# Chunked attention feeding a token and channel mixer: the loads of later q, k and v, the pairs' weight ring and the weights' sums move from SyncE's queue to ScalarE's

## The chip, the cores and the metric

The kernel runs on one core of a Trainium2 chip. The metric is the device time of one execution in microseconds (us), as the median of several runs. Below, PE is TensorE (PEld its weight loads), DVE is VectorE, ACT is ScalarE, POOL is GpSimd and SP is SyncE, which in this kernel issues DMAs and computes nothing.

## The reference

The batch is 8, with 8 heads, 576 positions and a head dimension of 64. Attention is taken within chunks of 64 positions, and its result is the input x (8 x 576 x 512) of a mixer without normalisation:

```python
scores = scale * np.matmul(q_c, k_c.transpose(0, 1, 2, 4, 3))   # chunks of 64
scores = scores - np.max(scores, axis=-1, keepdims=True)
attn = np.exp(scores)
attn = attn / (np.sum(attn, axis=-1, keepdims=True) + 1e-09)
out = np.matmul(attn, v_c)
...
xt = x.transpose(0, 2, 1)
h = np.maximum(xt @ w_tok1, 0.0) @ w_tok2        # 576 -> 256 -> 576
u = x + h.transpose(0, 2, 1)
h2 = np.maximum(u @ w_ch1, 0.0) @ w_ch2          # 512 -> 1536 -> 512
return (u + h2).astype(np.float32)
```

## The kernel before

**Precision.** Every operand of the mixer is held as a high part (a cast to the fast 32-bit matmul type) and a low part (what the cast left out), and each product is three matmuls: high x high, low x high, high x low. So a cast on ACT (`xh`, `rh`, `gh`, `bh`) is always followed by a subtraction on DVE or POOL (`xl`, `rl`, `gl`, `bl`).

**Stages.** The 4608 columns (batch x position) go through the channel MLP in blocks: first two halves of batch 0, then two single blocks of 512 columns, then three pairs of blocks. A pair uses a scheme with 7 products instead of 8, which needs sums and differences of the first channel weights. These sums are made on POOL (`add_sums`, L1017, into the one buffer `sparts`), split into high and low (`split_sums`: ACT L1023, POOL L1024), written to HBM as `w<-sparts` (`dump`, L881) and read back in the pairs through a ring of eight buffers (`load_product`, `ring<-w`, L1041), one load for each product on PE (L1051).

**Attention beside it.** The attention of later tiles (128 positions, 8 heads each) is cut into bursts that are put between the matmuls of the single blocks and of the first pairs. For one tile: `qk` and `v` are loaded (L304, L315) two bursts ahead; PE makes the scores (L372, beside the output product L384 of the tile two bursts earlier); DVE subtracts the maximum (L345, L348), ACT takes the exponential (`pr`, L352), DVE transposes 32 x 32 blocks (`blocks`, L395), and SP writes them to HBM (`far<-blocks`, L400) and reads them back rearranged (`pf<-far`, four DMAs, L406). ACT copies them to `pt` (L423), the weights of the output product L384. The tile's output x goes the same way: it is cast to `xh` (L483) and `xl` (POOL L484) for the token MLP (L581, `ps_t`; ACT `rh` L599, DVE `rl` L600; L653), and as blocks through HBM to `xt` (L406), the residual that DVE adds into `u` (L660).

**What sets the order.** PE's order and SP's order are written out by hand (SP issues in the order of the code). ACT, DVE and POOL are ordered by a scheduler, and some instructions are pinned behind another with `tc.issue_after`. All DMAs of the program, whoever issues them, take eight completion semaphores in turn; the issue of a DMA waits until the DMA eight places earlier, which holds the same semaphore, has landed.

Of the kernel before, what the change touches and what calls it, by code (L numbers as in the profile page):

```python
# [8 lines left out]
F32 = mybir.dt.float32  # L9
# [51 lines left out]
DUMPS = 2  # L61
# [46 lines left out]
def attention_mixer_kernel(ctx, tc, qk_in, vo_in, v_in, w1_in, w2_in, wc1_in, wc2_in, out):  # L108
# [19 lines left out]
    nc = tc.nc  # L128
# [170 lines left out]
            xts[k] = pool.tile([P, N // BK, NDT, BK], F32, tag="xt", name="xt")  # L299
        return xts[k]  # L300

    def load_qk(i):
        qk = pool.tile([P, 2, NHP, P], F32, tag="qk" if i > 4 else "qk0", name="qk", bufs=3 if i > 4 else 5)
        nc.sync.dma_start(out=qk.rearrange("p a b c -> p (a b c)"), in_=qk_in[i])  # L304
        tiles[i] = {"qk": qk}

    def load_v(i):
        if i < NTILE:
            v = pool.tile([P, VPAD], F32, tag="v1" if i > 4 else "v0", name="v", bufs=2 if i > 4 else 5)
            v = v[:, :VW].rearrange("p (a b c) -> p a b c", a=2, c=DV)  # L310
            src = vo_in[i]
        else:
            v = pool.tile([P, 2, NHP, D], F32, tag="v", name="v", bufs=4)
            src = v_in[i - NTILE]
        nc.sync.dma_start(out=v.rearrange("p a b c -> p (a b c)"), in_=src)  # L315
        tiles[i]["v"] = v

    def attn_load(i):
        load_qk(i)
        load_v(i)  # L320

    def attn_s(i, src=None, tag="at"):
        t = tiles[i]
# [17 lines left out]
    def attn_p(i, fill=0):  # L341
        t = tiles[i]
        sv = t["s"]
        mx = per_row("mx")
        nc.vector.tensor_reduce(out=mx, in_=sv, axis=AX.X, op=ALU.max)  # L345
        convert(fill)
        pr = t["pr"] = pool.tile([P, DM], F32, tag="pr", name="pr")
        nc.vector.tensor_tensor(  # L348
            out=pr.rearrange("p (h a k) -> p a h k", a=2, k=CH), in0=sv,
            in1=mx.broadcast_to([P, 2, NHP, CH]), op=ALU.subtract,  # L350
        )
        nc.scalar.activation(out=pr, in_=pr, func=AF.Exp, scale=1.0 / float(D) ** 0.5)  # L352

    def attn_z(i):

        t = tiles[i]
        zi = t["zi"] = per_row("zs")
        nc.vector.tensor_reduce(
            out=zi, in_=t["pr"].rearrange("p (h a k) -> p a h k", a=2, k=CH), axis=AX.X, op=ALU.add
        )  # L360
        nc.scalar.activation(out=zi, in_=zi, func=AF.Copy, bias=1e-9)
        nc.vector.reciprocal(out=zi, in_=zi)

    def attn_both(i, j):

        ps = ps_at.tile([P, 2, 512], F32, tag="at", name="ps_sv")
        if i is not None:
            qk = tiles[i]["qk"]
            for hp in range(NHP):
                for a in range(2):  # L370
                    for c in range(2):
                        nc.tensor.matmul(  # L372
                            ps[c * CH:(c + 1) * CH, a, hp * CH:(hp + 1) * CH],
                            lhsT=qk[a * D:(a + 1) * D, 0, hp, c * CH:(c + 1) * CH],
                            rhs=qk[a * D:(a + 1) * D, 1, hp, c * CH:(c + 1) * CH],
                            start=True, stop=True,
                        )
            tiles[i]["s"] = ps[:, :, :NHP * CH].rearrange("p a (h k) -> p a h k", k=CH)
        if j is not None:
            t = tiles[j]  # L380
            for hp in range(NHP):
                for a in range(2):
                    for c in range(2):
                        nc.tensor.matmul(  # L384
                            ps[c * CH:(c + 1) * CH, a, (NHP + hp) * D:(NHP + hp + 1) * D],
                            lhsT=t["pt"][a * CH:(a + 1) * CH, hp, c * CH:(c + 1) * CH],
                            rhs=t["v"][a * CH:(a + 1) * CH, c, hp, :D],
                            start=True, stop=True,
                        )
            t["pv"] = ps[:, :, NHP * D:2 * NHP * D].rearrange("p a (h d) -> p a h d", d=D)  # L390

    def far_out(src, tag="far"):

        blocks = pool.tile([P, DM], F32, tag="blocks", name="blocks")
        nc.vector.transpose(  # L395
            out=blocks.rearrange("p (g n c) -> p n g c", g=4, c=BK),
            in_=src.rearrange("p (n g c) -> p n g c", g=4, c=BK),
        )
        far = dram.tile([P, DM], F32, tag=tag, name="far", bufs=4 if tag == "far" else 24)
        nc.sync.dma_start(out=far, in_=blocks)  # L400
        return far
# [66 lines left out]
    def attn_end(i):  # L468
        t = tiles[i]
        if i % NTILE == 4 and i > 4:  # L470
            attn_stack(i)
        t["own"] = t["x"]
        t["x"] = far_out(t["x"], "far_x")
        close_tile(i)
# [12 lines left out]
    def batch_split(b):  # L487

        for t, _, _ in mix_tiles(b):
            attn_split(t)  # L490
            stack_end(t)
# [54 lines left out]
    def load_waiting(n):  # L546

        while waiting and n > 0:
            n -= load_x(*waiting.pop(0))
# [8 lines left out]
    def batch_tiles(b):  # L558
        base = (b // 2) * NTILE
        return [base + j for j in (range(0, 5) if b % 2 == 0 else range(5, 9))]  # L560
# [251 lines left out]
    for engine in engines:  # L812
        ins = [i for i in nc.cur_bb.bb.instructions if i.engine == engine][-1]
# [4 lines left out]
    order = [t for b in range(2, B) for t in sorted(batch_tiles(b), key=lambda t: t % NTILE != 4)]  # L818
# [55 lines left out]
    wide = ctx.enter_context(tc.tile_pool(name="wide", bufs=1, space=bass.MemoryType.DRAM))  # L874
    stored, tokens, dumps = {}, {}, []

    def dump(n):

        for key, src in dumps[:n]:
            stored[key] = wide.tile([P, 2, KH], F32, tag="w{}_{}".format(*key), name="w")  # L880
            nc.sync.dma_start(out=stored[key], in_=src if src.dtype == F32 else src.bitcast(F32))  # L881
        del dumps[:n]

# [47 lines left out]
    def attention(k):  # L931

        i = order[k] if k < len(order) else None
        j = order[k - LAG] if k >= LAG else None
        attn_both(i, j)
        if k + 2 < len(order):
            attn_load(order[k + 2])
        load_waiting(1)
        if i is not None:
            attn_p(i)  # L940
            tiles[i]["far"] = far_out(tiles[i]["pr"])
            attn_z(i)
        ready = len(waiting)
        if j is not None:
            attn_o(j)
            attn_end(j)
        load_waiting(min(2, ready))
# [88 lines left out]
    products = [(p, n) for _ in range(PAIRS) for p in range(NFC // 2) for n in range(7)]  # L1036

    def load_product(upto):
        for i in range(len(ring), min(upto, len(products))):
            w = pool.tile([P, 2, KH], F32, tag="ring", name="ring", bufs=RING)  # L1040
            nc.sync.dma_start(out=w, in_=stored[products[i]])  # L1041
            ring.append(w)

    def product(i, u, width):
# [211 lines left out]
    for k in range(SINGLE):  # L1256
        at, width = BLOCKS[k]
        accs, pend = [], None
        for f in range(NFC):
            for half in range(2):  # L1260
                if half == 0:
                    g = ch1(u, f, width=width)
                elif pend is not None:
                    ch2(*pend)
                if half == 1:
                    pend = (S + at, width, u, f, g, accs)
                now = 2 * (NFC * k + f) + half
                if now in TOKENS_AT:
                    b = 2 + TOKENS_AT.index(now)
                    batch_split(b)  # L1270
                    if b != 3:
                        load_waiting(99)
                    rs[b] = [tok1(b, m) for m in range(NT1)]
                if now in MIX_AT:
                    mix_pair(SINGLE, rs, MIX_AT.index(now))
                if now == OPEN_AT[0]:
                    open_x(1)
                if now == OPEN_AT[1]:
                    open_x(SINGLE, SINGLE + 1)
                if RING_AT <= now < RING_AT + RING - 1:  # L1280
                    load_product(now - RING_AT + 1)
                if now in TOKENS_TO:
                    store_token()
                for kind, at_k in single_events.get(now, ()):
                    calls[kind](at_k)
                dump(DUMPS)
                for p, (add, cut, put) in enumerate(SUMS):
                    for when, step in ((add, add_sums), (cut, split_sums)):
                        if now == when:
                            with in_turn():  # L1290
                                step(p)
                    if now == put:
                        dump_sums(p)
        dump(len(dumps) if k else 1)
        if k == 0:
            u = turn(1, rs)
        ch2(*pend)
# [57 lines left out]
```

## Time and profile before

| | |
|---|---|
| time, median of 3 runs | 741.4 us (740.5 to 743.21) |
| the profiled execution: its time, its span | 743.39 us, 741.4 us |
| mean granted clock of PE | 0.988 |
| PE / PEld busy | 97% / 85% |
| DVE / ACT / POOL busy | 59% / 37% / 26% |
| HBM traffic, mean over the span | 186 GB/s |
| DMAs' share of the sixteen engines | 57% |
| moved by the change: `ring<-w`, `w<-sparts`, later `qk`, later `v` | 126 of 256 KB, 24 of 256 KB, 25 of the 36 of 512 KB, 25 of the 27 of 256 KB |

The span runs from the first to the last instruction of the profiled execution. A busy share is an average over stages that are limited in different ways, so the rows below are read stage by stage. All hardware DMAs of the kernel before stand in one queue (q1 in the page's third part), which is SP's.

### The profile page before, as it was taken

How to read it: one execution, taken by the hardware profiler on the slowest of the kernel's cores; microseconds unless marked ns; L12 is line 12 of the kernel's file. 1: busy time of each engine (PE TensorE's matmuls, PEld its weight loads, DVE VectorE, ACT ScalarE, POOL GpSimd, SP SyncE). 2: the span in 40 equal slices, each digit the busy share in tenths (PEclk: the TensorE clock that was granted, in tenths of full speed). 3: DMA queues.
4: the chain of work that ended last, by engine and by line, in shares of the span. 5: the costliest groups of instructions: out<-in, count | busy, mean ns of one | idle time of the engine just before them, and what ended most of it. 6: DMA issues, size and time to landing. Idle time of an engine off the chain costs nothing.

```text
span 741.4 us, 14629 instructions
## 1 busy us (share of the span) xinstructions
PE 717.3 (97%) x5730; PEld 629.7 (85%) x5730; DVE 437.1 (59%) x735; ACT 275.4 (37%) x505; POOL 189.6 (26%) x161
## 2 busy tenths in 40 slices
PE   6899998999999999989999999999999999999997
PEld 4488898988889877878888888988888899999997
DVE  4799966555546546577666763686343539433361
ACT  5899953333332333332333333332211324112120
POOL 0000012162346543103111163061112602311220
PEclk8999999999999999999999999999999999999999
DMA  9956346669855676745888995045655430644111
GB/s 344 407 218 222 118 157 198 218 202 290 289 178 185 202 229 224 237 127 197 268 261 272 284 312 139 12 140 161 192 177 182 138 93 21 235 135 126 53 54 53
DMA packets 93268, 139.94 MB, mean 189 GB/s; under 512 B 10832, under 2 KB 44880, under 8 KB 93200
## 3 DMA queue, kind: packets, MB, share of 16 engines
q1 hardware_dynamic: 93200, 139.02, 57.0%
q8 instruction: 45, 0.74, 0.4%
q14 instruction: 23, 0.19, 0.1%
HBM read 98.34 MB, written 39.71 MB: 186 GB/s over the span
## 4 chain that ended last, share of the span: by engine, by line
PE 74%; DMA 8%; DVE 6%; ACT 5%; SPq 4%; issue 2%; POOL 0%; DVEq 0%; ACTq 0%; POOLq 0%
PE acc L1121 24%; PE ps_p L1051 21%; PE acc L726 8%; PE ps_c L682 7%; PE ps_t L653 5%; PE ps_t L581 4%; SPq L406 2%; DMA far<-blocks 2%; PE ps_sv L372 2%; PE ps_sv L384 1%; DMA raw_t<-in_w 1%; DVE wtop L225 1%; ACT low L206 1%; PE sum L590 1%; ACT wtop L205 1%
## 5 line engine op out<-in xcount | busy, mean ns | idle before, releaser
L1121 PE MATMUL acc<-gh,kept_c 128*128 128x512 f32 (+1 forms) x576 | 169.5, 376 | 0.0
L1051 PE MATMUL ps_p<-bh,ring 128*128 128x512 f32 (+1 forms) x504 | 148.5, 376 | 0.1
L1121 PEld LDWEIGHTS acc<-gh,kept_c 128*128 128x128 f32 x576 | 108.2, 189 | 12.8
L1121 PE MATMUL acc<-gl,kept_c 128*128 128x512 f32 (+1 forms) x288 | 107.9, 375 | 0.0
L1051 PEld LDWEIGHTS ps_p<-bh,ring 128*128 128x128 f32 x504 | 94.6, 189 | 11.8 <-DVE sum L1146 0.5
L1051 PE MATMUL ps_p<-bl,ring 128*128 128x512 f32 (+1 forms) x252 | 94.4, 375 | 0.0
L726 PE MATMUL acc<-gh,kept_c 128*128 128x288 f32 (+1 forms) x384 | 91.1, 341 | 1.7 <-ACT gh L695 1.5
L484 POOL TENSOR_TENSOR xl<-x,xh 128x512 fp32r<-128x512 f32 x28 | 37.7, 1358 | 160.4 <-ACT xh L483 137.2
L726 PEld LDWEIGHTS acc<-gh,kept_c 128*128 128x128 f32 x384 | 63.7, 192 | 8.2 <-ACT gh L695 2.8
L1148 POOL TENSOR_TENSOR sum<-snap,sum 128x512 f32<-128x512 f32 (+1 forms) x18 | 23.1, 1282 | 167.4 <-ACT snap L1140 144.7
L1121 PEld LDWEIGHTS acc<-gl,kept_c 128*128 128x128 f32 x288 | 54.4, 189 | 6.5
L682 PE MATMUL ps_c<-uh,kept_c 128*128 128x512 f32 x192 | 57.8, 383 | 1.3 <-DVE rl L600 1.3
L726 PE MATMUL acc<-gl,kept_c 128*128 128x288 f32 (+1 forms) x192 | 57.1, 336 | 0.0
L1051 PEld LDWEIGHTS ps_p<-bl,ring 128*128 128x128 f32 x252 | 47.6, 189 | 5.7
L1153 ACT ACTIVATE gh<-c 128x512 fp32r<-128x512 f32 (+1 forms) x36 | 22.4, 622 | 77.3 <-DVE c L1146 73.4
L352 ACT ACTIVATE pr<-pr 128x512 f32<-128x512 f32 x36 | 22.6, 628 | 76.6 <-DVE pr L348 76.6
L1140 ACT COPY snap<-ps_p 128x512 f32<-128x512 f32 (+1 forms) x36 | 20.8, 577 | 75.5 <-PE ps_p L1051 71.9
L1154 DVE SCALAR_TENSOR_TENSOR gl<-g,gh 128x512 fp32r<-128x512 f32 (+1 forms) x36 | 32.9, 936 | 24.4 <-ACT gh L1153 24.4
L696 DVE SCALAR_TENSOR_TENSOR gl<-ps_c,gh 128x512 fp32r<-128x512 f32 (+1 forms) x36 | 21.8, 605 | 40.1 <-ACT gh L695 40.0
L682 PE MATMUL ps_c<-both,kept_c 128*128 128x288 f32 x288 | 41.2, 291 | 1.0 <-DVE gl L696 1.0
L682 PEld LDWEIGHTS ps_c<-uh,kept_c 128*128 128x128 f32 x192 | 35.7, 189 | 6.8 <-DVE rl L600 1.7
L682 PEld LDWEIGHTS ps_c<-both,kept_c 128*128 128x128 f32 x288 | 37.2, 189 | 2.2 <-DVE gl L696 1.4
(134 smaller groups left out, 1257.8 us busy)
## 6 DMA issues: line engine op xcount, KB each, us to landing
ring<-w SPq DMA_DIRECT2D x126, 256.0 KB, 4.0
qk<-in_qk SPq DMA_DIRECT2D x36, 512.0 KB, 4.8
far<-blocks SPq DMA_DIRECT2D x63, 256.0 KB, 2.9
raw_c<-in_wc SPq DMA_DIRECT2D x24, 512.0 KB, 9.3
pf<-far SPq DMA_DIRECT2D x124, 64.0 KB, 2.4
v<-in_v SPq DMA_DIRECT2D x27, 256.0 KB, 4.6
xt<-far SPq DMA_DIRECT2D x96, 64.0 KB, 2.0
w<-sparts SPq DMA_DIRECT2D x24, 256.0 KB, 2.7
```

What stands on the lines that cost most here:

```text
L352: nc.scalar.activation(out=pr, in_=pr, func=AF.Exp, scale=1.0 / float(D) ** 0.5)
L484: nc.gpsimd.tensor_tensor(out=xl, in0=t["own"], in1=xh.bitcast(F32), op=ALU.subtract)
L581: nc.tensor.matmul(ps, lhsT=lhsT, rhs=in_turn_of_two(rhs), start=(n == 0 and q == 0), stop=(n == len(mt) - 1 and q == len(terms) - 1),)
L653: nc.tensor.matmul(ps[:, at:at + n], lhsT=lhsT[:, cols], rhs=rhs.rearrange("p (c a b) -> p c b a", a=2, b=RUN), start=(q == 0), stop=(q == ...
L682: nc.tensor.matmul(ps[:, :width], lhsT=weights["c1", f][:, wi, k // 2, k % 2 * P:(k % 2 + 1) * P], rhs=in_turn_of_two(u[ui][k]), start=(k ...
L696: nc.vector.scalar_tensor_tensor(out=halved(gl), in0=ps, scalar=0.0, in1=halved(gh.bitcast(F32)), op0=ALU.max, op1=ALU.subtract)
L726: nc.tensor.matmul(accs[e], lhsT=weights["c2", f][:, wi, e * P:(e + 1) * P], rhs=in_turn_of_two(g[gi]), start=(f == 0 and q == 0), stop=(f ...
L1051: nc.tensor.matmul(ps, lhsT=w[:, wi, j * P:(j + 1) * P].bitcast(F32R), rhs=in_turn_of_two(u[ui][j]), start=j == 0 and q == 0, stop=j == 1 ...
L1121: nc.tensor.matmul(accs[e], lhsT=weights["c2", f][:, wi, e * P:(e + 1) * P], rhs=in_turn_of_two(g[gi]), start=start and q == 0, stop=stop ...
L1148: engine.tensor_tensor(out=c, in0=a, in1=b, op=ALU.add)
L1153: nc.scalar.activation(out=gh, in_=c, func=AF.Relu)
L1154: nc.vector.scalar_tensor_tensor(out=gl, in0=c, scalar=0.0, in1=gh.bitcast(F32), op0=ALU.max, op1=ALU.subtract)
```

## The change

A new helper, `on_scalar`, pins what is recorded inside it behind the last ACT instruction recorded so far. `load_qk` and `load_v` take the queue as a parameter; the loads of tiles that the bursts bring, the dumps in the single blocks and every load of the ring are issued by `nc.scalar.dma_start` within `on_scalar`. The loads of the first tiles, `far`, `pf`, `xt`, `xc`, the token weights and the outputs stay with SP. No computing instruction is added or taken out.

```diff
+    def on_scalar():
+
+        ins = [i for i in nc.cur_bb.bb.instructions if i.engine == nc.scalar.engine][-1]
+        return tc.issue_after(ins)
+
-    def load_qk(i):
+    def load_qk(i, queue=nc.sync):
         qk = pool.tile([P, 2, NHP, P], F32, tag="qk" if i > 4 else "qk0", name="qk", bufs=3 if i > 4 else 5)
-        nc.sync.dma_start(out=qk.rearrange("p a b c -> p (a b c)"), in_=qk_in[i])
+        queue.dma_start(out=qk.rearrange("p a b c -> p (a b c)"), in_=qk_in[i])
...
-        nc.sync.dma_start(out=v.rearrange("p a b c -> p (a b c)"), in_=src)
+        queue.dma_start(out=v.rearrange("p a b c -> p (a b c)"), in_=src)
...
-    def dump(n):
+    def dump(n, late=False):
 
         for key, src in dumps[:n]:
             stored[key] = wide.tile([P, 2, KH], F32, tag="w{}_{}".format(*key), name="w")
+            if late:
+                with on_scalar():
+                    nc.scalar.dma_start(out=stored[key], in_=src if src.dtype == F32 else src.bitcast(F32))
+                continue
             nc.sync.dma_start(out=stored[key], in_=src if src.dtype == F32 else src.bitcast(F32))
...
         if k + 2 < len(order):
-            attn_load(order[k + 2])
+            with on_scalar():
+                attn_load(order[k + 2], nc.scalar)
...
             w = pool.tile([P, 2, KH], F32, tag="ring", name="ring", bufs=RING)
-            nc.sync.dma_start(out=w, in_=stored[products[i]])
+            with on_scalar():
+                nc.scalar.dma_start(out=w, in_=stored[products[i]])
...
-                dump(DUMPS)
+                dump(DUMPS, True)
...
-        dump(len(dumps) if k else 1)
+        dump(len(dumps) if k else 1, True)
```

The line numbers of the changed program are 5 to 11 higher in these functions: L304 is L309 there, L315 is L320, L352 is L357, L400 is L405, L406 is L411, L423 is L428, L483 is L488, L599 is L604, L881 is L888, L1023 is L1033 and L1041 is L1052.

**The first place, the sums near 255 us.** In SP's queue before, in the second single block, two dumps stand behind twelve DMAs that wait for the x of earlier tiles:

```order
L406 DMA xt<-far 32x4x128 x4
L400 DMA far<-blocks 128x512 x2
L406 DMA xt<-far 32x2x128 x4
L406 DMA xt<-far 32x4x128 x4
L881 DMA w<-sparts 128x512 x2
L406 DMA pf<-far 32x4x128 x4
```

In the changed program the same two dumps stand in ACT's queue, behind the `zs` of a burst and ahead of its `xh`, two `gh`, `pt` and the next cast of `sparts`:

```order
L366 ACTIVATE zs<-zs 128x8
L888 DMA w<-sparts 128x512 x2
L488 CAST xh<-x 128x512
L700 ACTIVATE gh<-ps_c_3650 128x512
L428 COPY pt<-pf 128x4x4x32
L700 ACTIVATE gh<-ps_c_3690 128x512
L309 DMA qk<-in_qk 128x1024
L320 DMA v<-in_v 128x512
L357 ACTIVATE pr<-pr 128x512
L509 CAST stack<-x 64x512 x2
L1033 CAST sparts<-sparts 128x4x256
```

So the dumps moved from behind the `xt` of SP to a place that only ACT's own work sets.

**The second place, SP at the end of the second single block (290 to 318 us).** Before, SP had three rounds of `far`, `pf` and `xt` with the moved DMAs between them:

```order
L400 DMA far<-blocks 128x512 x2
L406 DMA pf<-far 32x4x128 x4
L304 DMA qk<-in_qk 128x1024
L315 DMA v<-in_v 128x512
L406 DMA xt<-far 32x4x128 x4
L400 DMA far<-blocks 128x512 x2
L1041 DMA ring<-w 128x512
L406 DMA pf<-far 32x4x128 x4
L1041 DMA ring<-w 128x512
L881 DMA w<-sparts 128x512 x2
L1041 DMA ring<-w 128x512
L304 DMA qk<-in_qk 128x1024
```

(behind them `v`, and then the last `xt`, four pieces of 32 KB). In the changed program SP's queue holds there:

```order
L405 DMA far<-blocks 128x512 x2
L411 DMA pf<-far 32x4x128 x4
L411 DMA xt<-far 32x4x128 x4
L405 DMA far<-blocks 128x512 x2
L411 DMA pf<-far 32x4x128 x4
L411 DMA xt<-far 32x2x128 x4
L405 DMA far<-blocks 128x512 x2
```

The six transfers that stood right ahead of the last `xt` (`32x2x128`) are gone from it, and so are `qk` and `v` one round earlier.

**The third place, ACT at the same time (298 to 307 us).** Before, ACT's queue held only work there, from the second of the round's `gh` to its `zs`: `gh`, `pt`, `pr`, `xh`, `gh`, `zs`. In the changed program, with what each row waits for (DMAHWn is one of the eight DMA semaphores, the others are engines' counters):

```order
L1052 DMA ring<-w 128x512 [waits DMAHW6_49]
L428 COPY pt<-pf 128x4x4x32 [waits DMAHW1_49,DMAHW3_49,DMAHW0_49,Activation_49]
L888 DMA w<-sparts 128x512 [waits DMAHW2_49,Pool_49]
L888 DMA w<-sparts 128x512 [waits DMAHW4_49]
L1052 DMA ring<-w 128x512 [waits DMAHW6_49]
L309 DMA qk<-in_qk 128x1024 [waits DMAHW0_49,PE_49]
L320 DMA v<-in_v 128x512 [waits DMAHW1_49]
L357 ACTIVATE pr<-pr 128x512 [waits DVE_49]
L488 CAST xh<-x 128x512 [waits DVE_49]
L700 ACTIVATE gh<-ps_c_4244 128x512 [waits PE_49]
```

What moved: `pr` and `xh`, which followed `pt` directly, now follow six DMAs, and each of these waits for the DMA that held its semaphore before. Counted off in the order of issue, the one that `v` waits for is the first piece of the last `xt` of the SP listing above.

## Rows read from the trace of the kernel before

**Rows 1.** First part of the page: busy time, share and instructions of each engine.

```profile
PE 717.3 (97%) x5730; PEld 629.7 (85%) x5730; DVE 437.1 (59%) x735; ACT 275.4 (37%) x505; POOL 189.6 (26%) x161
```

**Rows 2.** Windows: length, then PE, PEld, DVE, ACT, POOL busy, PEclk, DMA share, GB/s.

```profile
270.00:285.00 15.00, 12.75 (x160) 10.38 (x162) 8.87 (x14) 7.00 (x13) 7.83 (x6) 1.00 0.75 242
325.80:329.20 3.40, 3.40 (x16) 3.40 (x16) 2.37 (x5) 0.62 (x1) 1.60 (x1) 0.50 0.00 0
330.00:705.00 375.00, 374.92 (x2517) 332.25 (x2516) 212.08 (x322) 106.58 (x190) 95.96 (x71) 1.00 0.53 168
```

**Rows 3.** Timeline, 257 to 274 us: start, duration, instruction [idle before <-releaser].

```profile
257.96 0.61 ACT L423 COPY pt<-pf 128x512 f32<-128x512 f32 x1
...
264.18 2.11 SPq L881 DMA_DIRECT2D w<-sparts  x2
...
268.44 1.42 POOL L1017 TENSOR_TENSOR sparts<-wsum 128x256 f32<-128x256 f32 x2 [8.19 <-DMA w<-sparts]
...
271.39 1.04 ACT L1023 CAST sparts<-sparts 128x1024 fp32r<-128x1024 f32 x1 [4.22 <-POOL sparts L1017]
...
272.45 1.07 ACT L599 ACTIVATE rh<-ps_t 128x512 fp32r<-128x512 f32 x2
...
273.81 0.70 PE L682 MATMUL ps_c<-uh,kept_c 128*128 128x512 f32 x2 [1.27 <-DVE rl L600]
```

**Rows 4.** Timeline of ACT and PE, 283 to 285 us.

```profile
283.17 0.60 ACT L695 ACTIVATE gh<-ps_c 128x512 fp32r<-128x512 f32 x1
283.90 0.21 ACT L361 ACTIVATE zs<-zs 128x8 f32<-128x8 f32 x1
...
284.73 0.69 PE L384 MATMUL ps_sv<-v,pt 64*64 64x64 f32 x32 [0.97 <-ACT pt L423]
```

**Rows 5.** Timeline of SP's queue, 290 to 313 us.

```profile
290.86 0.85 SPq L400 DMA_DIRECT2D far<-blocks  x2
295.99 1.74 SPq L406 DMA_DIRECT2D pf<-far  x4
297.83 0.38 SPq L304 DMA_DIRECT2D qk<-in_qk  x1
...
298.74 1.84 SPq L406 DMA_DIRECT2D xt<-far  x4
300.68 0.85 SPq L400 DMA_DIRECT2D far<-blocks  x2
...
305.55 1.74 SPq L406 DMA_DIRECT2D pf<-far  x4
307.39 0.38 SPq L1041 DMA_DIRECT2D ring<-w  x1
...
310.39 2.40 SPq L406 DMA_DIRECT2D xt<-far  x4
```

**Rows 6.** Chain that ended last, 285 to 330 us: start, duration, what.

```profile
290.86 5.08 DMA far<-blocks
...
300.68 4.85 DMA far<-blocks
...
312.37 5.76 DMA xt<-far
```

**Rows 7.** Timeline of ACT, POOL, PE and DVE, 302 to 326 us.

```profile
302.60 0.63 ACT L352 ACTIVATE pr<-pr 128x512 f32<-128x512 f32 x1 [2.27 <-DVE pr L348]
...
304.01 1.27 POOL L484 TENSOR_TENSOR xl<-x,xh 128x512 fp32r<-128x512 f32 x1 [3.08 <-PE ps_c L682]
...
306.08 0.38 PE L581 MATMUL ps_t<-xl,kept_t 128*128 128x512 f32 x1
...
318.31 0.69 DVE L660 TENSOR_TENSOR u<-ps_t,xt 128x512 f32<-128x512 f32 x1 [4.04 <-DMA xt<-far]
...
325.20 0.46 PE L653 MATMUL ps_t<-kept_t,rh 128*128 128x192 f32 x2 [3.14 <-DVE u L660]
```

**Rows 8.** DMA issues of the whole span: count, KB each, median us to landing.

```profile
far<-blocks SPq DMA_DIRECT2D x63, 256.0 KB, 2.9
...
xt<-far SPq DMA_DIRECT2D x52, 32.0 KB, 3.0
```

**Rows 9.** SP's waits: total us, times, longest.

```profile
SPq L1041 <- PE ps_p L1051: 57.7, 26, 8.0
```

More of the change, by code (lines that the diff above doesn't have):

```diff
@@ L300, in block_x, with load_v @@
         return xts[k]
-    def load_qk(i):
+    def on_scalar():
+        ins = [i for i in nc.cur_bb.bb.instructions if i.engine == nc.scalar.engine][-1]
+        return tc.issue_after(ins)
+    def load_qk(i, queue=nc.sync):
         qk = pool.tile([P, 2, NHP, P], F32, tag="qk" if i > 4 else "qk0", name="qk", bufs=3 if i > 4 else 5)
-        nc.sync.dma_start(out=qk.rearrange("p a b c -> p (a b c)"), in_=qk_in[i])
+        queue.dma_start(out=qk.rearrange("p a b c -> p (a b c)"), in_=qk_in[i])
         tiles[i] = {"qk": qk}
-    def load_v(i):
+    def load_v(i, queue=nc.sync):
         if i < NTILE:
@@ L314, in load_v, with attn_load @@
             src = v_in[i - NTILE]
-        nc.sync.dma_start(out=v.rearrange("p a b c -> p (a b c)"), in_=src)
+        queue.dma_start(out=v.rearrange("p a b c -> p (a b c)"), in_=src)
         tiles[i]["v"] = v
-    def attn_load(i):
-        load_qk(i)
-        load_v(i)
+    def attn_load(i, queue=nc.sync):
+        load_qk(i, queue)
+        load_v(i, queue)
     def attn_s(i, src=None, tag="at"):
```

## The prediction

> **What bounds the kernel now.** The first part of the page says that PE is busy 97% of the span and every other engine 59% or less [rows 1]. PE's order and instructions are untouched, so the change can only take away or add time in which PE waits. The windows show where that time lies: in the 375 us of the pairs PE is busy 374.92 us at full clock, so nothing is to be won there, only lost [rows 2]. The end of the second single block is left, and the timeline shows three waits in it. Near 272 us PE waits 1.27 us for `rl` [rows 3]. At 284.73 it waits 0.97 us for `pt` [rows 4]. At 325.20 it waits 3.14 us for `u`, and the windows show what follows: in the 3.4 us after it the granted clock is 0.50, the 1.2 GHz level, although PE is busy all the time, while after the two shorter waits the clock stays 1.00 [rows 2, 7]. So the third wait costs 3.14 us and half of 3.4, that is 1.7 us more.
>
> **What the change gives.** *Near 272 us.* Reading back from PE: `rl` follows `rh`, `rh` stands in ACT's queue behind the cast of `sparts`, the cast follows POOL's sums, and POOL had waited 8.19 us for the dump that frees the one `sparts` buffer; that dump left SP only at 264.18 [rows 3]. In the changed order it stands on ACT ahead of the `pt` that ran at 257.96, so it goes 6 us earlier, POOL and the cast are done long before `rh`, and the wait of 1.27 us goes.
>
> *At 284.73.* One `qk` issue of about 0.4 us comes between `gh` at 283.17, whose next instruction could start about 0.5 us later, and `zs` at 283.90 [rows 4, 5]; `zs` and `pt` behind it come about 0.2 us later, and PE with them: +0.2. Both together: PE and all that follows it come 1.27 - 0.2 = 1.1 us earlier.
>
> *At 325.20.* `u` waited 4.04 us for `xt` [rows 7]. In SP's queue the last `xt` was issued at 310.39, behind six transfers of which the first went out at 307.39 [rows 5], and its last piece took from 312.37 for 5.76 us [rows 6]. All six are moved, so `xt` is issued at least 3.0 us earlier and behind less traffic. The wait of 3.14 us and the slow 1.7 us behind it go, if nothing on ACT takes their place: -4.84.
>
> **What the change costs.** The third listing of the change shows it: on ACT, `pr` and `xh` now stand behind `v`, whose issue waits until the first piece of that last `xt` has landed. Queued behind `v` are `pr`, `xh`, then POOL's `xl`, and PE's `ps_t<-xl` at 306.08. From `pr` at 302.60 to the end of `xl` at 305.28 is 2.68 us, 0.8 us ahead of PE [rows 7]. So ACT becomes part of a chain that runs through SP and HBM. I follow it from the same `far` at 290.86, which landed in 5.08 us [rows 5, 6]. (The 2 us that SP gains ahead of it I leave to the range, since its `blocks` and the same traffic ahead remain.)
> - `pf` x4 from 295.99, 1.74 us. `qk` and `v` no longer follow, so `xt` x4, then 1.84 us, starts at 297.8, not at 298.74, and the next `far` goes at 299.7, not at 300.68 [rows 5].
> - Its flight of before, 4.85 us, is kept [rows 6]: the `qk`, `v` and `xt` ahead of it are on their way still. Landed at 304.6.
> - `pf` x4, 1.74 us, then `xt`: issued at 306.4, not at 310.39.
> - The flight of `xt` is not known. Below stands the median for pieces of 32 KB, 3.0 us [rows 8]; above the 5.76 us of before [rows 6]. I take 3.0, since the transfers that stood right ahead of it are now spread over ACT's waits. Landed at 309.4.
> - `v` is issued by 309.8 (0.44 us like one of the `pf`), `xl` ends 2.68 us later, at 312.5. The chain began with a burst on PE, which comes 1.1 us earlier: 311.4.
>
> PE reaches 306.08 in the old count, so it goes on 5.3 us later than before, after waits of 6.4 us in all, some of them at the `pt` of the bursts on the way, which follow `ring` and dump issues with waits of the same kind. The 3.14 us were followed by a slow stretch, so I let this wait have one too: +1.7, which cancels the 1.7 that goes.
>
> **In the pairs** I charge nothing. There ACT is busy 106.58 of 375 us [rows 2]; some 120 ring loads and 13 each of `qk` and `v` at 0.44 us add 64 us, less than half in all. A ring load waits for the product that frees its buffer: 57.7 us of waiting on SP [rows 9], now ACT's, but the copy behind it waits for a product too. If this cover fails, a `pt` comes late by one issue in each of some 13 bursts: up to 13 x 0.44 = 5.7 us more, which only the upper end holds.
>
> **Sum**: +5.3 (the gate on ACT, the 1.1 us earlier start included) - 3.14 (`u`) - 1.7 + 1.7 (slow stretches) = +2.2 us. The profiled execution took 743.4 us, 2.0 more than the median; 745.6 would be its new time, and against the median of 741.4 the sum gives 743.6. A measurement of this kernel can tell about 0.5%, 3.7 us, from no change, so this is no change.
>
> **Rivals.**
> *A, the gate opens in time.* What speaks for it is that SP is relieved of all large transfers, and the median flight of `far` is 2.9 us, not 5 [rows 8]. With 2.9, 2.9 and 3.0 the chain lands the last `xt` at 305.2 and `xl` ends at 307.2, 1.1 us late: 1.1 - 4.84 = -3.7, or 737.7 us; with no lateness, -1.1 - 4.84, 735.5. Against it: both `far` stood near 5 us with exactly this traffic ahead.
> *B, slower: the flights stay long.* If the last `xt` takes 5.76 us [rows 6] after 306.4, `xl` ends at 314.2, 8.1 us late: 8.1 - 3.14 = +5.0, 746.4 us, with `pt` waits in the pairs up to 749 and a little beyond. It decides when `xt` lands after 311.0 (a lateness of 6.9 us, which is 3.7 + 3.14), that is with a flight over 4.6 us. For it speaks that DMAs run 0.75 of the time in the stretch from 270 us on [rows 2], and that the loads on ACT, no longer held back by SP's order, meet the `xt` on the way. The Trainium skill, page "DMA: Bandwidth & Descriptors", section "Issuing engines are not separate DMA queues", says that DMAs of several issuing engines run on the same 16 DMA engines and interleave, and that issuing from several saves only the sequencer's issue time. By that rule the flights stay as they were, which is B's time; the trace of before, with one hardware queue, can't show it.
> *C, the chain as forecast*, 739 to 745: +2.2 with either slow stretch counted or not, and flights of `xt` from 2 to 4.6 us.
>
> **How the numbers follow.** C 0.49, A 0.18, B 0.33 (it has the bound of the pairs on its side too). A is faster by over 0.5%, C within it, B slower. The range goes from a little under A with its short flights, 737, to B with `pt` waits in the pairs, 749.
>
> **What would show it.** In the changed trace: no idle time of PE before `ps_c` at about 272 us, POOL's sums begin soon after 258; `u` no longer waits for `xt`, and the clock holds 1.00 at 325. In their place PE waits at `ps_t<-xh` or `ps_t<-xl` (L586) near 305 to 311 for ACT `xh` or POOL `xl`, and ACT's idle time before `pr` (L357) is put down to a DMA or to its own queue. A is right if that wait is under 2.5 us, B if it is over 8. I am wrong altogether if a wait in the pairs (`pt` before L389, `snap` or `gh` before L1062) holds more than 3 us, if an issue costs ACT much more than 0.44 us, or if the loads that now run ahead of SP's transfers delay an early `far` and PE waits before 250 us.

## The result: 749.0 us, 1.0% slower

The changed kernel took 749.0 us (median of 6 runs, 746.15 to 751.21), the kernel before 741.21 us beside it (6 runs, 740.28 to 743.21): a ratio of 1.0101, with a 95% interval of 1.007 to 1.0131. That is the upper end of the forecast range, 737 to 749, and it is the time of rival B; the likeliest case, no change, did not come about. The profiled execution of the changed kernel has a span of 748.7 us against 741.4 before.

PE's waits in the changed kernel (engine, line, what it waited for: total us, times, longest):

```profile
PE ps_sv L389 <- ACT pt L428: 6.1, 4, 2.1
...
PE ps_t L586 <- ACT xh L488: 3.6, 1, 3.6
...
PE acc L731 <- DVE gl L701: 0.8, 1, 0.8
```

The waits for `u` and `rl` [rows 3, 7] are no longer among PE's waits. What stands in their place is `pt`, four times, and `xh`, both of ACT. The timeline of PE has them one by one (start, duration, instruction, idle time before it and who ended it):

```profile
197.49 0.48 PE L731 MATMUL acc<-gl,kept_c 128*128 128x512 f32 x1 [0.77 <-DVE gl L701]
...
201.77 0.69 PE L389 MATMUL ps_sv<-v,pt 64*64 64x64 f32 x32 [1.22 <-ACT pt L428]
...
274.87 0.59 PE L687 MATMUL ps_c<-uh,kept_c 128*128 128x512 f32 x2
...
285.61 0.69 PE L389 MATMUL ps_sv<-v,pt 64*64 64x64 f32 x32 [0.89 <-ACT pt L428]
...
294.43 0.69 PE L389 MATMUL ps_sv<-v,pt 64*64 64x64 f32 x32 [2.12 <-ACT pt L428]
...
305.58 0.69 PE L389 MATMUL ps_sv<-v,pt 64*64 64x64 f32 x32 [1.86 <-ACT pt L428]
...
314.62 1.22 PE L586 MATMUL ps_t<-xh,kept_t 128*128 128x512 f32 x2 [3.61 <-ACT xh L488]
```

PE's order is the same in both kernels, so each of its matmuls can be set against the same one before, and the lag read at each wait. The `pt` product at 201.77 ran at 199.32 before: +2.4, nearly all of it new. The `ps_c` at 274.87 ran at 273.81 [rows 3]: the lag falls to +1.1, since the wait of 1.27 us is gone. The lag is +3.2 at 294.43, +5.2 at 305.58 and +9.0 at 314.62. Behind it PE runs slowly for 6.8 us, as the windows show (length, busy PE, PEld, DVE, ACT, POOL, granted clock, DMA share, GB/s):

```profile
314.60:318.00 3.40, 3.25 (x7) 2.17 (x8) 2.07 (x5) 1.02 (x3) 1.27 (x1) 0.50 1.02 387
318.00:321.40 3.40, 3.40 (x10) 2.68 (x9) 0.69 (x1) 0.25 (x1) 0.00 (x0) 0.51 0.66 211
321.40:324.80 3.40, 3.40 (x25) 3.27 (x24) 1.26 (x2) 0.60 (x1) 0.00 (x0) 1.00 0.00 0
```

Two stretches of 3.4 us at half clock, where I had counted one, bring the lag to +12.6. Then the place where PE waited for `u` comes, and it waits no longer: +9.3, and with the slow stretch of before gone too [rows 2], +7.6 and at the end +7.3, the difference of the spans.

The chain that ended last shows how ACT came to be 9 us late (283 to 316 us; pieces under 0.1 us are left out):

```profile
284.23 4.87 DMA far<-blocks
289.24 0.32 SPq L411
...
294.29 5.57 DMA far<-blocks
299.99 0.32 SPq L411
...
303.73 3.96 DMA far<-blocks
307.75 3.81 DMA pf<-far
311.58 0.33 ACTq L888
311.95 0.45 ACTq L1052
312.49 0.41 ACTq L309
312.94 0.44 ACTq L320
313.43 0.63 ACT pr L357
314.06 0.52 ACT xh L488
314.65 1.28 POOL xl L489
315.97 0.79 PE ps_t L586
```

It runs through three rounds of SP's `far` and `pf`, and then into ACT's queue: `pf` lands, a dump (L888) can go, then a ring load, `qk`, `v`, and only then `pr`, `xh`, `xl` and PE. ACT's own timeline has the place where it stood (ACTq is its issuing):

```profile
306.11 5.80 ACTq L888 DMA_DIRECT2D w<-sparts  x2
...
312.94 0.44 ACTq L320 DMA_DIRECT2D v<-in_v  x1
313.43 0.63 ACT L357 ACTIVATE pr<-pr 128x512 f32<-128x512 f32 x1 [7.90 <-issue]
```

Two dumps, each of 0.4 us on SP, took 5.80 us on ACT, because the second waited; ACT was idle for 7.90 us ahead of `pr`, against 2.27 before [rows 7].

### The profile page after: what moved, and what is told of

Read it like the earlier page. It is cut to its first block, busy times and chain, and to the rows that moved or that the text cites. A ratio compares the mean times of both kernels' runs of the same rounds, so it can differ in the third digit from the quotient of the medians.

```text
span 748.7 us, 14535 instructions
## 1 busy us (share of the span) xinstructions
PE 720.5 (96%) x5730; PEld 631.2 (84%) x5730; DVE 439.2 (59%) x735; ACT 274.8 (37%) x505; POOL 188.8 (25%) x161
## 3 DMA queue, kind: packets, MB, share of 16 engines
q1 hardware_dynamic: 64400, 80.02, 31.9%
q10 hardware_dynamic: 28800, 59.00, 25.2%
## 4 chain that ended last, share of the span: by engine, by line
PE 74%; DMA 10%; ACT 6%; DVE 4%; SPq 2%; issue 2%; ACTq 1%; POOL 0%; DVEq 0%
PE acc L1132 24%; PE ps_p L1062 22%; PE ps_t L658 6%; PE ps_c L687 6%; PE ps_t L586 6%; PE acc L731 5%; DMA far<-blocks 3%; DMA pf<-far 3%; SPq L411 2%; PE ps_sv L377 1%; PE ps_sv L389 1%; PE sum L595 1%; ACT low L206 1%; ACT wtop L205 1%; DMA raw_t<-in_w 1%
## 5 line engine op out<-in xcount | busy, mean ns | idle before, releaser
L357 ACT ACTIVATE pr<-pr 128x512 f32<-128x512 f32 x36 | 22.6, 629 | 90.8 <-DVE pr L353 43.9
```

## The experiments

Three theories. **W**: ACT's queue stands still because its DMA issues wait for earlier transfers to land (the turn of eight semaphores is shared with SP), and `pr`, `pt` and `xh` stand behind them. **I**: the time that ACT spends on the issues costs. (There are 200 of them: 126 for the ring, 24 dumps, 25 `qk` and 25 `v`. The 175 that some of the expectations name leave 25 out.) **L**: loads in a second queue run ahead of SP's order and lengthen the flights of `far`, `pf` and `xt`. Each ratio is against runs of the kernel before on the same chip, whose median was 738.6 to 740.0 us in these; it need not be the quotient of the two medians. e1 to e6 had 4 runs each, the others 10 to 12.

| run | what is where | median us | ratio, 95% interval |
|---|---|---|---|
| e1 | all DMAs on SP, dummy work on ACT | 742.66 | 1.0029, 0.9991 to 1.0067 |
| e2 | only the dumps on ACT | 740.99 | 1.0011, 0.9972 to 1.005 |
| e3 | only `qk` and `v` on ACT | 749.67 | 1.0129, 1.0088 to 1.017 |
| e4 | only the ring on ACT | 741.73 | 1.0015, 0.9972 to 1.0058 |
| e5 | `qk` and `v` on ACT, behind `pr`, `xh`, `zs` | 747.51 | 1.0106, 1.0071 to 1.014 |
| e6 | the whole change, `qk` and `v` as in e5 | 750.58 | 1.0132, 1.0104 to 1.0159 |
| e7 | only `qk` and `v`, on POOL | 738.62 | 0.9974, 0.9953 to 0.9994 |
| e8 | dumps and ring on ACT | 743.7 | 1.0058, 1.0034 to 1.0082 |
| e9 | all DMAs on SP, a wait on ACT | 745.84 | 1.0089, 1.0066 to 1.0112 |
| e10 | `qk` and `v` on POOL, early dumps on ACT | 737.92 | 1.0003, 0.9978 to 1.0028 |
| e11 | all that is moved on POOL | 741.83 | 1.0042, 1.0017 to 1.0068 |
| e12 | only the early dumps on ACT | 736.71 | 0.9969, 0.9942 to 0.9995 |

### The time of the issues (e1)

```diff
+    def on_scalar(n=1):
+        for _ in range(n):
+            ins = [i for i in nc.cur_bb.bb.instructions if i.engine == nc.scalar.engine][-1]
+            with tc.issue_after(ins):
+                nc.scalar.copy(out=warm_in, in_=warm_in)
```

It is called once ahead of each dump in the single blocks and each ring load, and twice ahead of `qk` and `v`; the DMAs stay on SP. `warm_in` isn't used any more at that time.

> All DMAs stay in SyncE's queue as before; ScalarE gets one small in-place copy (128x288) pinned at each place where the change issues a DMA, two for a pair of qk and v, so it loses about the time of the issues but waits for no transfer. Theory W (ScalarE's queue stands still because its DMA issues wait for earlier transfers to land, and pr, pt and xh stand behind them): nearly nothing, 740 to 744 us; the 3.14 us wait for u and the 1.27 us wait stay, the 0.97 us wait for pt grows by up to 0.5. Theory I (the time of 175 issues on ScalarE is what costs): the loss returns, 746 to 751 us, with waits for pt, pr or xh on PE at about the same places as in the changed kernel.

Measured: 742.66 us, a ratio whose interval holds 1. The copies took 432 ns each (median), as long as an issue, and PE's later waits stayed those of before: 2.4 us for `u`, 1.2 for `rl`, 0.9 for `pt`. Theory I falls: 0.4 us at every one of these places costs 0.7% at the most, by the interval, and no new wait of PE is seen. The copies are pinned as the issues are, so the pinning by itself is not what costs either.

### The parts alone (e2, e3, e4)

e2 keeps the `nc.scalar` of the dumps only, e3 that of `qk` and `v`, e4 that of the ring; the other two are issued by `nc.sync` as before, as here in e2:

```diff
-            with on_scalar():
-                attn_load(order[k + 2], nc.scalar)
+            attn_load(order[k + 2])
...
-            with on_scalar():
-                nc.scalar.dma_start(out=w, in_=stored[products[i]])
+            nc.sync.dma_start(out=w, in_=stored[products[i]])
```

> Only the 24 dumps of the sums go to ScalarE; ring, qk and v stay with SyncE. Theory W: the wait of 1.27 us near 272 goes; the dumps near 306 wait on ScalarE ahead of pr and xh for transfers of SyncE, which has kept its ring, qk and v, so part of the wait at ps_t<-xh can be there (0 to 5 us): 738 to 744 us. Theory I: 24 issues of 0.4 us beside idle time, and the 1.27 us gone: 739.5 to 741 us, with no wait at ps_t<-xh. Theory L (what hurts is that loads on a second queue run ahead and lengthen the flights of far, pf and xt): the dumps are writes of 6 MB in all, 740 to 742.

> Only the 25 later qk and 25 later v go to ScalarE; dumps and ring stay with SyncE. Theory W: pr stands behind v in each burst, so the waits at 195 to 202 (about 2.4 us in the changed kernel) and at 294, 305 and 314 (2.1, 1.9, 3.6 us) stay in good part, and the 1.27 us wait is not taken away: 745 to 752 us. Theory I: 50 issues, under a third of the change's: 741 to 744 us. Theory L: qk and v are 19 MB that run ahead: 744 to 750 us with flights of pf near 3.8 us, as W; the two differ in ScalarE's rows, whether pr stands behind a v that waits.

> Only the 126 loads of the ring go to ScalarE. Theory W: three ring loads near 300 to 312 stand ahead of gh, pt and pr and wait for transfers of SyncE; in the pairs a ring load waits for a product that the copy behind it waits for too: PE loses at most 1 to 3 us near 305 and nothing in the pairs, and u's wait of 3.1 us shrinks by 1 to 2: 739 to 744 us. Theory I: 126 of the 175 issues, so most of the loss: 745 to 749 us, in the pairs too.

Measured: dumps alone 1.0011 and ring alone 1.0015, neither told from 1; `qk` and `v` alone 1.0129, as much as the whole change lost. e3 falls as W and L have it, and the ring, with 126 of the 200 issues, speaks once more against I. In e3's timeline of ACT:

```profile
305.83 0.34 ACTq L309 DMA_DIRECT2D qk<-in_qk  x1
314.14 0.34 ACTq L320 DMA_DIRECT2D v<-in_v  x1
314.58 0.63 ACT L357 ACTIVATE pr<-pr 128x512 f32<-128x512 f32 x1 [8.61 <-DMA pf<-far]
```

and of PE, a little later:

```profile
315.77 0.70 PE L586 MATMUL ps_t<-xh,kept_t 128*128 128x512 f32 x2 [4.22 <-ACT xh L488]
```

`v` follows `qk` only 8.3 us later, when a `pf` has landed; its buffer was not what it waited for (its listing names a DMA semaphore alone); ACT was idle for 8.61 us ahead of `pr`. Dumps and ring do the same on a smaller scale: in e2 PE waits 2.3 us for `xh`, in e4 3.2 us for `pt`, and the 1.27 us (e2) and the 3.14 us with the slow stretch (both) that they save pay for it.

### A better place for qk and v (e5, e6)

```diff
         i = order[k] if k < len(order) else None
...
-        if k + 2 < len(order):
-            with on_scalar():
-                attn_load(order[k + 2], nc.scalar)
...
             attn_z(i)
+        if k + 2 < len(order):
+            with on_scalar():
+                attn_load(order[k + 2], nc.scalar)
         ready = len(waiting)
```

e5 is e3 with this, e6 the whole change with it.

> The same 25 qk and 25 v on ScalarE as in the run with qk and v alone (749.7 us), dumps and ring with SyncE; the loads are recorded behind the burst's pr, xh and zs instead of ahead of them. The issues still wait for the same kind of transfers, but pr and xh are in front. Theory W: the waits of xh at 315 and of pt at 297 and 305 go; what still stands behind a waiting v is the next pt or rh, a burst later: 739 to 744 us. Theory L (the loads on a second queue meet far, pf and xt and lengthen them): place in ScalarE's order does not matter, 746 to 751 us.

> The whole change, with qk and v behind pr, xh and zs of their burst; dumps and ring stay on ScalarE where the change put them. Theory W: of the 7.8 us the part that qk and v cause goes, what the dumps and the three ring loads near 300 to 312 do by their waits ahead of pt and pr stays (sums alone gave 1.8 us of lateness at 308, ring alone 1.5 us at 302): 740 to 746 us. Theory L: 747 to 752 us.

Measured: 1.0106 and 1.0132. My expectation from W missed both times; taken alone, these two speak for L. The rows of e6 say where the loss went, first ACT's timeline:

```profile
293.42 0.35 ACTq L309 DMA_DIRECT2D qk<-in_qk  x1
293.86 1.04 ACTq L320 DMA_DIRECT2D v<-in_v  x1
295.31 0.62 ACT L428 COPY pt<-pf 128x512 f32<-128x512 f32 x1 [3.83 <-DMA xt<-far]
```

and then PE's waits:

```profile
PE ps_sv L389 <- ACT pt L428: 9.0, 8, 2.3
```

`xh` is no longer late (0.6 us), but now `pt` stands behind the loads and waits with them: eight waits of PE, 9.0 us. In a burst ACT has `pt`, `pr`, `xh` and `zs` to do, PE wants each in time, and in both of the places tried the waiting loads held one of them up.

### The wait without the loads, and the loads without the wait (e9, e7)

e9 moves nothing. At the place where the change issues `qk` and `v`, ACT copies eight columns of the newest `pf` into `warm_in`:

```diff
+    newest = []
+
+    def wait_for_pf():
+
+        if newest:
+            ins = [i for i in nc.cur_bb.bb.instructions if i.engine == nc.scalar.engine][-1]
+            with tc.issue_after(ins):
+                nc.scalar.copy(out=warm_in[:, :8], in_=newest[0].rearrange("p a b c -> p (a b c)")[:, :8])
...
             attn_load(order[k + 2])
+        wait_for_pf()
...
             far_in(t.pop("far"), t["pf"])
+            newest[:] = [t["pf"]]
```

> Every DMA stays in SyncE's queue as before. At the place in each burst where the change issues qk and v, ScalarE gets one tiny copy (128x8) of the newest pf, so that it waits there until the four pf have landed, as the issue of v did in the run with qk and v alone; no transfer is moved. Theory W (a wait for SyncE's transfers ahead of pr and xh is what costs): pf lands near 309 where pr ran at 302.6, so xh is 5 to 7 us late there and pt or xh in other bursts 1 to 2: 745 to 753 us, with PE waiting for ACT xh at ps_t. Theory L (the moved loads' traffic on a second queue costs): nothing is moved, 740 to 743 us.

Measured: 1.0089, interval 1.0066 to 1.0112; in the middle of what W has and outside of what L has. ACT's timeline, with the copy in L938:

```profile
289.42 0.60 ACT L695 ACTIVATE gh<-ps_c 128x512 fp32r<-128x512 f32 x1 [0.44 <-PE ps_c L682]
297.80 0.20 ACT L938 CAST warm_in<-pf 128x8 bf16<-128x8 f32 x1 [7.78 <-DMA pf<-far]
297.90 0.62 ACT L352 ACTIVATE pr<-pr 128x512 f32<-128x512 f32 x1
```

and PE's:

```profile
302.07 0.69 PE L384 MATMUL ps_sv<-v,pt 64*64 64x64 f32 x32 [3.00 <-ACT pt L423]
```

ACT stands idle for 7.78 us ahead of a copy of 0.20 us, and `pr` runs at 297.90, where it ran at 293.52 before; the `pt` behind it is then late for PE. The waits came as `pt` rather than as the `xh` that I had named. In this execution the wait at 302.07 is paid back where PE doesn't wait for `u` any more: set matmul against matmul with the kernel before, PE is 1.4 us ahead at 291 us, 3.5 behind at 306 (a slow stretch follows the wait) and 1.3 ahead at 329. What stays is a second wait of the same kind, in the pairs, and a stretch of 3.4 us at a granted clock of 0.51 after it (ACT's timeline and PE's):

```profile
420.39 0.20 ACT L938 CAST warm_in<-pf 128x8 bf16<-128x8 f32 x1 [6.99 <-DMA pf<-far]
...
422.16 0.69 PE L384 MATMUL ps_sv<-v,pt 64*64 64x64 f32 x32 [2.33 <-ACT pt L423]
```

From there on PE is 2.6 us behind. By the two ratios, a wait alone costs about two thirds of what `qk` and `v` on ACT cost (0.89% and 1.29%; the intervals overlap).

e7 is e3 with POOL in ACT's place:

```diff
-        ins = [i for i in nc.cur_bb.bb.instructions if i.engine == nc.scalar.engine][-1]
+        ins = [i for i in nc.cur_bb.bb.instructions if i.engine == nc.gpsimd.engine][-1]
...
-                attn_load(order[k + 2], nc.scalar)
+                attn_load(order[k + 2], nc.gpsimd)
```

> The 25 qk and 25 v are issued by GpSimd instead of ScalarE, pinned behind GpSimd's last instruction; dumps and ring stay with SyncE. In the listing these loads take a turn of eight semaphores of their own (DMASW) and wait mostly for PE or for a load of their own kind that is long done. Theory W: no pr or pt stands behind a transfer, so the waits at 297, 305 and 315 are gone; GpSimd's xl can be late by an issue: 738 to 745 us. Theory L: the same bytes run on a second queue beside far, pf and xt: 746 to 751 us, with pf's median flight at 3.4 us or more.

Measured: 738.62 us, 0.9974, no loss (the interval ends at 0.9994, just under 1). In the listing of e7 the loads on POOL have eight semaphores to themselves, so the eight that all DMAs take in turn "whoever issues them" are those of SP and ACT only. POOL issues both loads in 1.1 us:

```profile
301.61 0.55 POOL L309 DMA_DIRECT2D qk<-in_qk  x1
302.16 0.54 POOL L320 DMA_DIRECT2D v<-in_v  x1
306.20 1.28 POOL L489 TENSOR_TENSOR xl<-x,xh 128x512 fp32r<-128x512 f32 x1 [3.51 <-PE ps_c L687]
```

The flights of `pf` are as long as in e3, 3.5 and 3.4 us (median of 124) against 2.4 before, and PE waits 1.36 us at 169.07 and 0.72 us at 293.51 for `pt`, where it did not before. So with the loads on a second queue `pf` flies longer, as L has it, and some 2 us of PE's waiting can be put down to that; it is not what made the change slow, since the same traffic without the waits on ACT gave a ratio of 0.9974 where e3 gave 1.0129. (ACT and POOL differ in more than the semaphores; that the wait itself costs rests on e9.)

### Combinations (e8, e10, e11, e12)

e8 is the change with `attn_load(order[k + 2])` on SP; e12 is e2 with `dump(DUMPS, now < 40)` in place of `dump(DUMPS, True)`; e10 is e7 with the early dumps of e12 (19 of its 20; the one behind the loop stays with SP); e11 is the change with `nc.gpsimd` in `on_scalar` and at the three places of issue.

> Dumps and ring on ScalarE, qk and v with SyncE: the change without its qk and v. Theory W: the dumps and one ring load near 303 to 308 stand ahead of pr and xh and wait for pf and xt of SyncE, so part of the lateness stays: 2 to 5 us at ps_t<-xh, against the 1.3 us and the 3.1 + 2.0 us that go: 739 to 744 us. Theory I (issue time): 150 of 175 issues, 746 to 748 us.

> Only the dumps of the sums issued before step 40 of the single blocks are on ScalarE; everything else as before. Theory W: the 1.27 us wait goes and the lateness of 1.8 us that the late dumps gave near 308 in the run with all dumps does not come; u's wait stays at about 3 us: 738.5 to 740.5 us. If dumps cost ScalarE anything there by their issue (theory I): 740 to 742 us.

> qk and v on GpSimd as in the run that gave 738.6 us, and of the sums those dumps on ScalarE that are issued before step 40 of the single blocks (the later ones and the ring with SyncE). Theory W: the 1.27 us wait near 272 goes as well, and the dumps near 306 no longer stand ahead of pr: 736 to 739 us, 0.2 to 0.6% under the kernel before. Theory L: the pf flights stay near 3.5 us and the waits for pt at 169 and 293 (about 2.5 us) with them; the same time, as it holds only those.

> All that the change moves to ScalarE goes to GpSimd instead: ring, dumps, qk and v, each pinned behind GpSimd's last instruction. ScalarE issues nothing. Theory W: the waits for xh and pt behind DMA issues are gone; what can be late is GpSimd's own xl, bl and sum behind a ring load that waits for PE, so 737 to 746 us and at any rate less than the change's 749.0. Theory L: 747 us or more, as the bytes on the second queue are those of the change.

Measured: e8 1.0058, in W's range: dumps and ring together cost 0.58%, where neither could be told from nothing alone (the intervals overlap, so that together they cost more than the sum of the two is not shown); in its profiled execution PE waits up to 4.1 us for `pt`, near 301. e12 0.9969, faster by 0.05 to 0.58%, the lowest of all: the 1.27 us is gone and no late dump stands ahead of `pr`. I had thought that `u` would go on waiting; in the profiled execution it didn't, and the row is gone from PE's waits; why is not shown. e10 1.0003: the two gains don't add up. Its interval overlaps those of e7 and e12, which end at 0.9994 and 0.9995, so whether either gain is real stays open; its profile has the shortest span but one, 735.2 us. e11 1.0042, under the change's 1.0101 as W has it. `pf` flies 2.7 us there (median), with all the bytes of the change on the second queue, so these bytes alone don't lengthen it. One wait that e11 adds lies in the pairs:

```profile
PE ps_sv L377 <- DVE sum L1157: 1.8, 1, 1.8
```

Not tried: giving ACT's loads semaphores of their own.

## Why the prediction was half right

**Right: the time, in part by luck.** 749.0 us is the upper end of the range, and that end was B with waits for `pt` in the pairs. Those did not come: PE is busy 110.00 of 110 us and 160.00 of 160 from 330 to 600 us, as the forecast's own sum had it. Nor did B's condition hold in its own way. `xt` did land after 311.0, but because it was issued at 310.27 instead of 306.4; its pieces flew 1.8 to 3.1 us, close to the 3.0 that I took, against 5.8 to 7.1 before, and B needed more than 4.6. By the sign that I gave, the one wait at `ps_t`, 3.61 us, it is neither A (under 2.5) nor B (over 8). Another sign, PE waiting before 250 us, came true at 201.77. (C's lower end, 739, does not come out of its own terms: a flight of 2 us and no new slow stretch give 740.9.)

**Right: the mechanism of the cost**, a chain through `far`, `pf` and SP into ACT's DMA issues with `pr` and `xh` behind. In the changed trace it decides, piece by piece.

**Right in number, wrong in mechanism: what goes.** The waits of 1.27 us and for `u` are gone, but not in the way worked out. *Near 272 us* the dump did leave early, at 259.20 against 264.18, but the cast of `sparts` and `rh` came later than before [rows 3], since they stand on ACT behind a `pr` that now waits for `qk` and `v`:

```profile
269.68 0.34 ACTq L320 DMA_DIRECT2D v<-in_v  x1
270.12 0.63 ACT L357 ACTIVATE pr<-pr 128x512 f32<-128x512 f32 x1 [4.38 <-DMA pf<-far]
...
271.91 1.05 ACT L1033 CAST sparts<-sparts 128x1024 fp32r<-128x1024 f32 x1
...
272.98 0.58 ACT L604 ACTIVATE rh<-ps_t 128x512 fp32r<-128x512 f32 x1
```

PE doesn't wait for `rl` because it comes there 2.4 us late itself. Where `qk` and `v` stay with SP, in e2, the mechanism works as forecast: the cast runs at 267.04 and `rh` at 269.45, with PE in time until then. *The wait for `u`*: `xt` was issued at 310.27, hardly earlier than the 310.39 of before, and only its flight was shorter. PE came 12.6 us late and would have found even the `xt` of before landed [rows 7]. The issue on SP in the changed kernel:

```profile
310.27 2.27 SPq L411 DMA_DIRECT2D xt<-far  x4
```

**Wrong: the size of the gate, 5.3 us forecast, 9.0 found at 314.62** (`ps_t<-xl`, which the forecast was for, runs right behind it at 315.97, +9.9). `xl` ended at 315.93 and not at 311.4.
- *The start.* This is the step that failed: it makes 4.5 us, the whole difference. I kept `far` at 290.86 and took 1.1 us off at the end; it went at 294.29, so 3.4 and 1.1 us later. The round before had already been slow: its `far` was issued 0.9 us later than before and flew for 4.87 us, while before it was issued at 283.33 and `pf` could follow at 285.92; the `xt` behind it took 3.05 us to issue, where those of before took 1.85. In the changed kernel `qk` (284.14) and `v` (285.88) go out beside this `far`, which SP's order used to put behind it; the two dumps stood beside it before as well. That fits theory L, a part of rival B, in the place where I had left only an earlier start to the range, but no run separates it here. And PE was not 1.1 us early, as the forecast has it, but 0.9 us late at 285.61.
- *The flights.* 5.57 and 3.96 us came instead of 5.08 and 4.85, about what I took. But the last step was not the flight of `xt` of 3.0 us. The dump ahead of `v` waited for the first piece of the last `pf` to land, 3.81 us after 307.75; I had followed `v`'s semaphore only, and each of the six DMAs ahead of `pr` has one. This made 0.5 us: `v` was out 5.7 us after `far` had landed, where I had 5.2.
- *Other bursts.* A gate of the same kind is what made PE late so early. At 194 us `v` waited on ACT and ACT was idle for 8.46 us ahead of `pr`:

```profile
193.92 0.34 ACTq L320 DMA_DIRECT2D v<-in_v  x1
194.30 0.63 ACT L357 ACTIVATE pr<-pr 128x512 f32<-128x512 f32 x1 [8.46 <-DMA pf<-far]
```

That gave +2.4 us by 201.77. I had looked for gates only near those places where PE had waited before.

**Wrong: the slow stretch**: 1.7 us counted, 3.6 measured (+9.0 to +12.6). The forecast +2.2 and the measured +7.3 differ by 3.7 (the gate) and 1.9 (the stretch), less 0.2, since the wait for `u` with its stretch gave back 5.06 us where I had counted 4.84, and less 0.3 that came back later.

The Trainium skill's rule that issuing from several engines saves only issue time and leaves the transfers on the same 16 engines (page "DMA: Bandwidth & Descriptors", section "Issuing engines are not separate DMA queues") agrees with the traces: the packets of the two queues of the changed kernel take 31.9% and 25.2% of the sixteen engines' span, where the one queue of before took 57.0%, and in e3 and e7 the flights of `pf` became longer, not shorter. What the issues cost on ACT is not their time (e1) but their waits (e9).

## What to carry to other kernels

A DMA put into a computing engine's queue brings its waits with it: look at each semaphore that its issue waits for, and at what stands behind it in that queue, not at the 0.4 us of the issue. Copies of 0.4 us in the places of the issues cost nothing that could be told (e1); copies of 0.2 us that wait for a transfer cost 0.9% (e9). If loads must leave a full queue, give them to an engine with slack behind them (e7; there they also had semaphores of their own, and which of the two counts is not shown), and move only those that are late for something, as the early dumps were (e12, whose gain is only just clear of nothing). And where a wait has gone, look whether its cause came earlier or the waiting engine came later: in the changed kernel PE was late, and nothing was won.

## What the hardware showed that I had not expected

After the wait of 3.14 us at 325 before, the clock was at half for 3.4 us [rows 2]; after the wait of 3.61 us at 314.62 it was so for 6.8 us, at 0.50 and 0.51. A wait of much the same length need not be followed by a slow stretch at all. In the kernel before, PE waited 1.98 us for `pt` at 123.89 and the granted clock was 0.50 from 124.4 to 127.8; in the changed kernel it waited 2.12 us for `pt` at 294.43, and there the window reads

```profile
294.40:297.80 3.40, 3.37 (x45) 2.98 (x46) 2.58 (x4) 0.48 (x1) 1.41 (x2) 1.00 0.72 150
```

at full clock. And in e12, where PE waited 1.63 us at the first of these places, it reads

```profile
124.40:127.80 3.40, 3.40 (x55) 3.19 (x54) 2.51 (x4) 1.80 (x4) 1.28 (x1) 1.00 1.07 396
```

Whether such a stretch is slow moves a whole execution by about 1.7 us, a part of the spread of up to 7.75 us within a kernel's runs (e12), so that two profiles alone don't rank two kernels here.
